# Attention and two expert layers: key tails of two heads in one chunk, sums of values 65 columns a head, and another planned order

## Chip, cores and metric

The kernel runs on one core of a Trainium2 chip. The metric is the device time of one execution in microseconds (us), lower is better. Engines: PE (TensorE matmuls), DVE (VectorE), ACT (ScalarE), POOL (GpSimd), SP (SyncE, which issues most DMAs).

## The reference, cut to what matters

```python
def _attn_ref(q, k, v, omega):          # q, k, v: 4 batches, 8 heads, 576 tokens, 64 wide; omega: 128 x 64
    scale = 1.0 / np.sqrt(np.sqrt(D))
    q_s, k_s = (q * scale, k * scale)
    def phi(x):
        h = np.einsum('bhsd,md->bhsm', x, omega) - np.sum(x * x, axis=-1, keepdims=True) / 2.0
        h = h - np.max(h, axis=-1, keepdims=True)
        return np.exp(h) / np.sqrt(m)
    q_p, k_p = (phi(q_s), phi(k_s))
    kv = np.einsum('bhsm,bhsd->bhmd', k_p, v)
    z = np.sum(k_p, axis=2)
    num = np.einsum('bhsm,bhmd->bhsd', q_p, kv)
    den = np.einsum('bhsm,bhm->bhs', q_p, z)[..., None] + 1e-06
    return num / den
```

Its result, as 2304 rows of 512, goes through two layers of eight experts (512 to 1024, ReLU, back to 512), each row through the expert with the largest gate.

## The kernel before, in words

**Attention** goes by 16 pairs of heads, four to a batch (`class Pair`, L298). A pair's steps are:

- `load_q`, `load_k`, `load_v` (L312 to L340): the inputs, with two heads on the 128 partitions;
- `k_proj` with `features` (L360, L465): keys against omega, 128 tokens at a time, five chunks a head of which the last overlaps the fourth; ten fp32 products with 64 rows each, two heads side by side, into four PSUM banks (tile `ph`); then `nm`, the maximum by DVE, and ten ACT exponentials into `kp`;
- `kv` (L471): for each head five products of `kp` with the values `vt` into `pkv`. A column of ones among the values makes the sum of keys. Three pairs (form R) take 65 columns a head, the others 128;
- `q_split` and `q_proj` (L391, L409): queries against omega. In batches 0 and 1 ("tiled") one load brings both heads and four 64-row fp32 products make both; in batches 2 and 3 each head has a load of its own, is cut into two fp32r parts by a DVE cast and a DVE subtraction, and takes four fp32r products (`pa<-qs`). POOL then makes a maximum over partitions;
- `q_exp`, `q_cut` and `num` (L440, L457, L499): exponentials, and their product with `kv`. Form F keeps fp32 (two matmuls a head, `pa<-qhh,kvr`), form S cuts both sides into fp32r parts (six a head, `qh`, `ql`, `kvh`, `kvl`), form R writes rows instead of columns (`pn`);
- `den_a` to `norm`: division, by way of a small DMA round trip.

An fp32 product shows as two records in the trace, an fp32r product as one.

**Experts.** A `Unit` (L836) is one batch in one layer, with the expert that most of the batch takes. `up` and `down` run 384 fp32r products of 288 columns each (`pm`), eight units in a row: the order is batch 0, batch 1, both in layer 0, then both in layer 1, and the same with batches 2 and 3. Between groups of six such products, at a `slot`, PE takes pieces of attention and of the gates (`gate`, L729: `pg`, `pt`, `pc`, `ptc`). A `Block` gathers 32 rows that need another expert (`pst`, `pxt`, `pu` and others) during the last two units.

**What sets the order.** The program is recorded once, and everything stands in a fixed order on each engine. `Attention.go` (L680) picks the next step by a table of weights (`WEIGHTS`, `RAW_WEIGHTS`, `TWEAKS`, `PACE`), out of those that `Estimate` (L101), a rough clock that runs along, holds to be ready. Where nothing is ready before the first unit, `fill` (L1316) lays down a matmul on zeros (`idle`). From the first unit on, attention and gates share four PSUM banks (`psa`), the units hold the other four (`psm`); ahead of it there are seven. `ORDERS`, `FORMS` and `COPIES` say which unit comes when, which form a pair has, and whether ACT or DVE makes a copy. What is recorded for one engine is worked off strictly in turn.

Of the kernel before, what the change touches and what calls it, by code (L numbers as in the profile page):

```python
# [11 lines left out]
F32 = mybir.dt.float32  # L12
# [13 lines left out]
NCH = 5  # L26
SP = NCH * 128
# [12 lines left out]
MODES = "AAAA"  # L40

TILED = "1100"
# [11 lines left out]
FORMS = "FRRRFFFSSSSSSSSS"  # L54
# [3 lines left out]
WEIGHTS = (-99.0, -99.0, 262.75, -267.46, 198.55, 332.25, -310.29, -471.44, -33.14, 239.82, -489.57, 351.55, -254.05, 173.97)  # L58
RAW_WEIGHTS = (-99.0, -99.0, -374.05, -379.93, 519.94, 42.51, 947.74, -153.49, 153.44, 733.35, -182.45, -952.4, -419.2, -198.78)
# [8 lines left out]
START_PACE = (0.142, 0.015, 7.433)  # L68
START_COPIES = (1, 2, 0, 1, 0, 0, 0)
TWEAKS = {  # L70
    ("den_a", 1): 44.7, ("den_a", 2): 595.6, ("den_a", 3): -18.8, ("den_a", 4): 323.2, ("den_a", 5): 525.4,
    ("den_a", 6): 291.8, ("den_a", 7): -101.8, ("den_a", 8): -71.9, ("den_a", 9): 56.6, ("den_b", 0): 325.6,
    ("den_b", 1): 1.1, ("den_b", 4): 37.9, ("den_b", 5): -9.0, ("den_b", 6): 171.8, ("den_b", 7): 121.2,
    ("den_b", 8): -64.0, ("den_b", 9): -127.0, ("den_c", 0): 75.6, ("den_c", 1): -98.6, ("den_c", 2): 478.0,
    ("den_c", 4): 37.6, ("den_c", 5): -237.6, ("den_c", 6): -550.8, ("den_c", 9): 0.0, ("den_w", 0): 345.4,
    ("den_w", 1): 143.8, ("den_w", 2): 574.5, ("den_w", 3): -16.2, ("den_w", 4): -57.6, ("den_w", 5): -71.8,
    ("den_w", 6): 77.2, ("den_w", 7): 20.5, ("den_w", 8): 24.7, ("den_w", 9): 7.5, ("k_proj", 0): 107.5,
    ("k_proj", 1): -20.1, ("k_proj", 2): 135.6, ("k_proj", 3): -98.0, ("k_proj", 4): -29.4,
    ("k_proj", 5): -51.0, ("k_proj", 6): -49.7, ("k_proj", 8): 473.1, ("k_proj", 9): -623.2, ("kv", 0): -176.7,
    ("kv", 1): -125.4, ("kv", 3): 483.1, ("kv", 4): -62.8, ("kv", 7): -51.7, ("kv", 8): -203.5,  # L80
    ("kv", 9): 650.0, ("norm", 0): 643.8, ("norm", 1): 542.2, ("norm", 2): 77.4, ("norm", 3): -45.2,
    ("norm", 4): -186.2, ("norm", 5): -106.9, ("norm", 6): 227.5, ("norm", 7): 48.0, ("norm", 8): -0.4,
    ("norm", 9): -5.1, ("num", 0): 0.5, ("num", 1): -19.9, ("num", 10): 26.1, ("num", 14): 416.8,
    ("num", 16): 22.8, ("num", 17): 45.6, ("num", 18): 55.1, ("num", 2): -74.7, ("num", 3): 19.4,
    ("num", 4): -844.8, ("num", 6): 170.0, ("num", 7): -558.5, ("q_cut", 1): -198.8, ("q_cut", 11): -85.3,
    ("q_cut", 12): 60.3, ("q_cut", 13): -72.2, ("q_cut", 14): -1186.5, ("q_cut", 16): -207.1,
    ("q_cut", 17): 478.9, ("q_cut", 19): -174.8, ("q_cut", 2): 25.9, ("q_cut", 3): -306.2, ("q_cut", 4): -287.7,
    ("q_cut", 5): -24.0, ("q_cut", 6): -93.1, ("q_cut", 7): -533.3, ("q_cut", 9): -21.1, ("q_exp", 0): -237.5,
    ("q_exp", 1): 916.5, ("q_exp", 10): -245.4, ("q_exp", 11): -365.4, ("q_exp", 13): -179.8,
# [11 lines left out]
class Estimate:  # L101
# [3 lines left out]
    def __init__(self):  # L105
        self.now = dict.fromkeys(("tensor", "vector", "scalar", "gpsimd", "sync", "dma"), 0.7)
        self.written, self.used, self.slots, self.before = {}, {}, {}, {}
        self.sums = set()

        self.window, self.work, self.slow = 0, 0.0, True  # L110

        self.hold = 0.0
# [1377 lines left out]
```

## Time and profile before

| | |
|---|---|
| median of 3 runs | 588.97 us (588.17 to 589.77) |
| profiled execution | 588.86 us, of which the span on the core 587.1 us |
| PE busy | 567.9 us, 97% of the span |
| DVE, ACT, POOL busy | 371.1, 225.3, 68.4 us |
| first expert product | 71.87 us after the start |
| idle matmuls | 54 |

A busy PE is not a PE at its peak: records overlap, so the price of a group is the distance from its start to the next group's start. What stands in brackets in a row of the timeline is idle time of that engine before the row, and what ended it.

### The profile page before, as it was taken

Reading aid. Unit: us, or ns where it says so; the run is one execution under the profiler, and the core shown is the slowest. Engines: PE = TensorE matmul, PEld = TensorE weight load, DVE = VectorE, ACT = ScalarE, POOL = GpSimd, SP = SyncE. Lnnn points to the kernel's source line nnn. Section 1 sums busy time; section 2 is a strip of 40 time slices with the busy share of each in tenths; the row PEclk is TensorE's granted clock in tenths of the full one; section 3 lists DMA queues with packets and bytes.
Section 4 is the critical chain, followed back from the end, with each engine's and each line's share of the span. In section 5 each row is a group of like instructions: output and inputs, shape, how many; then the busy total and the mean of one; then the engine's idle time right before and its main releaser. Section 6 shows DMA issues by size and latency. Waiting matters only on the chain.

```text
span 587.1 us, 11426 instructions
## 1 busy us (share of the span) xinstructions
PE 567.9 (97%) x4519; PEld 540.7 (92%) x4519; DVE 371.1 (63%) x695; ACT 225.3 (38%) x503; POOL 68.4 (12%) x48
## 2 busy tenths in 40 slices
PE   8999989999999999999999999999999999999995
PEld 7887779988999999899999999999999999879995
DVE  4487678887775787487866876764545485313522
ACT  6776645224536224424353344322331232324300
POOL 3670500202001130011201210000000000000000
PEclk9999999989999999999999999999999999999998
DMA  9314376525473263283534634544243238664411
GB/s 315 105 62 129 93 231 194 155 87 171 127 171 123 80 217 89 66 272 130 177 94 124 199 103 114 137 150 136 81 118 133 93 95 250 235 218 154 122 41 45
DMA packets 96955, 82.76 MB, mean 141 GB/s; under 512 B 24576, under 2 KB 78464, under 8 KB 96896
## 3 DMA queue, kind: packets, MB, share of 16 engines
q1 hardware_dynamic: 95776, 81.78, 45.1%
q8 instruction: 37, 0.61, 0.4%
q10 hardware_dynamic: 1120, 0.19, 0.2%
q14 instruction: 22, 0.18, 0.1%
HBM read 66.36 MB, written 15.54 MB: 140 GB/s over the span
## 4 chain that ended last, share of the span: by engine, by line
PE 80%; DVE 8%; DMA 5%; issue 3%; ACT 2%; POOL 0%; SPq 0%; ACTq 0%; DVEq 0%; POOLq 0%
PE pm L208 62%; PE pkv L208 5%; PE ph L208 4%; PE pa L208 4%; DMA wr<-w1a 2%; DVE qhh L208 1%; PE pg L208 1%; DMA wr<-w2a 1%; DVE wl L208 1%; DMA qr<-qT 1%; DVE nm L208 1%; ACT wh L208 1%; PE pby L208 1%; DMA rdd<-dt 1%; ACT kp L208 1%
## 5 line engine op out<-in xcount | busy, mean ns | idle before, releaser
L208 PE MATMUL pm<-xh,wh 128*128 128x288 f32 x512 | 113.4, 303 | 1.6 <-DVE hl L208 1.3
L208 PE MATMUL pm<-hh,wh 128*128 128x288 f32 x512 | 114.2, 302 | 0.6 <-DVE y L208 0.6
L208 PE MATMUL pm<-hh,wl 128*128 128x288 f32 x512 | 111.4, 297 | 0.0
L208 PE MATMUL pm<-hl,wh 128*128 128x288 f32 x512 | 111.3, 297 | 0.0
L208 PE MATMUL pm<-xh,wl 128*128 128x288 f32 x512 | 109.6, 296 | 0.5 <-DVE wl L208 0.5
L208 PE MATMUL pm<-xl,wh 128*128 128x288 f32 x512 | 109.5, 295 | 0.0
L208 POOL PARTITION_ALL_REDUCE qhl<-qhh x32 | 67.2, 2139 | 282.8 <-DVE qhh L208 185.2
L208 ACT CAST wh<-wr 128x1024 fp32r<-128x1024 f32 (+1 forms) x72 | 67.8, 951 | 55.5 <-PE pm L208 40.5
L208 PEld LDWEIGHTS pm<-xh,wh 128*128 128x128 f32 x512 | 82.1, 189 | 5.7 <-DVE hl L208 2.3
L208 PEld LDWEIGHTS pm<-hh,wh 128*128 128x128 f32 x512 | 82.9, 190 | 4.4 <-issue 3.0
L208 DVE TENSOR_TENSOR wl<-wr,wh 128x1024 fp32r<-128x1024 f32 (+1 forms) x72 | 78.5, 1103 | 12.6 <-ACT wh L208 12.2
L208 PEld LDWEIGHTS pm<-hh,wl 128*128 128x128 f32 x512 | 83.3, 190 | 0.0
L208 PEld LDWEIGHTS pm<-hl,wh 128*128 128x128 f32 x512 | 83.2, 190 | 0.0
L208 DVE SCALAR_TENSOR_TENSOR hl<-pm,hh 128x576 fp32r<-128x576 f32 x64 | 48.4, 757 | 54.8 <-ACT hh L208 53.9
L208 PEld LDWEIGHTS pm<-xh,wl 128*128 128x128 f32 x512 | 82.4, 188 | 0.7 <-DVE wl L208 0.7
L208 PEld LDWEIGHTS pm<-xl,wh 128*128 128x128 f32 x512 | 82.3, 188 | 0.0
L208 ACT ACTIVATE hh<-pm 128x576 fp32r<-128x576 f32 x64 | 41.7, 651 | 73.3 <-PE pm L208 73.2
L208 DVE TENSOR_TENSOR y<-pm,cb 128x576 f32<-128x576 f32 (+1 forms) x33 | 24.3, 737 | 58.4 <-PE pm L208 58.3
L208 ACT ACTIVATE kp<-ph,nm 128x128 f32<-128x128 f32 x140 | 38.0, 387 | 21.1 <-DVE nm L208 19.2
L208 ACT ACTIVATE qhh<-qhh 128x576 f32<-128x576 f32 x32 | 22.1, 706 | 58.3 <-DVE qhh L208 56.1
L208 DVE TENSOR_REDUCE nm<-ph 128x3 f32<-128x384 f32 (+1 forms) x64 | 27.2, 484 | 14.2 <-PE ph L208 14.1
L208 PEld LDWEIGHTS pkv<-vt,kp 128*128 128x128 f32 x280 | 32.6, 192 | 1.5 <-ACT ev L208 0.8
(145 smaller groups left out, 580.0 us busy)
## 6 DMA issues: line engine op xcount, KB each, us to landing
wr<-w2a SPq DMA_DIRECT2D x16, 512.0 KB, 4.1
wr<-w2b SPq DMA_DIRECT2D x16, 512.0 KB, 3.9
qr<-qT SPq DMA_DIRECT2D x24, 288.0 KB, 4.3
wr<-w1a SPq DMA_DIRECT2D x12, 512.0 KB, 4.7
wr<-w1b SPq DMA_DIRECT2D x12, 512.0 KB, 3.9
vt<-vp SPq DMA_DIRECT2D x16, 325.0 KB, 4.5
kr<-kT SPq DMA_DIRECT2D x16, 288.0 KB, 4.4
xd<-xraw SPq DMA_DIRECT2D x16, 288.0 KB, 3.5
```

Of the source, the lines that this page charges most:

```text
L208: return f(*args, **kw)
```

## The change

- The last 64 keys of both heads form one chunk: `kT` is laid out with 640 columns, the tail of head 0 on the first 64 partitions and that of head 1 on the others, with zeros elsewhere. `features` makes eight products with 64 rows and one with 128, into three banks; `nm` is made by three reductions, and nine exponentials follow.
- `kv` makes one product of 130 columns for the shared chunk and eight of 65, all into one group of sums; the copies that follow are 130 wide.
- All batches are "tiled": one query load a pair, four 64-row fp32 products, no `q_split`.
- Four pairs (8, 9, 11, 15 of 0 to 15) go from form S to form F.
- `Estimate` follows which PSUM bank will come free next, and prices DMAs and PE's activity otherwise. `go` takes a step only where as many of the shared banks as it needs have a reader recorded: four for `q_proj`, three for `k_proj`, two for `num`, one for `kv`.
- All weights and paces are other numbers; copies go to other engines (`COPIES`). The gates write two exponentials into tiles of their own.

```diff
-NCH = 5
+NCH = 4
+KW = NCH * 128 + 128
-TILED = "1100"
+TILED = "1111"
-FORMS = "FRRRFFFSSSSSSSSS"
+FORMS = "FRRRFFFSFFSFSSSF"
-PACE = (0.097, 0.001, 1.054, 1.126, 886.024, 3.696, 0.265, 0.264, 1.069, 256.941, 0)
-COPIES = (1, 1, 2, 1, 0, 0, 2)
+PACE = (0.168, 0.007, 0.458, 0.787, 1760.614, 1.248, 1.538, 0.278, 0.307, 366.477, 149.2)
+COPIES = (1, 0, 0, 1, 0, 0, 0)
-START_COPIES = (1, 2, 0, 1, 0, 0, 0)
+START_COPIES = (0, 0, 0, 2, 0, 1, 2)
...
+    def spare(self, pool, tag):
+        ring = id(pool), tag
+        return pool.bufs - sum(n not in self.seen or self.seen[n][1] for n in self.slots.get(ring, ()))
...
         def features(self, x, out):
-            parts = [(cs, self.heads(len(cs) * NF)) for cs in ((0, 1, 2), (3, 4))]
+            parts = [(ps, slice(NCH * j, NCH * j + NCH)) for j, ps in enumerate(self.heads(NCH * NF))]
+            for c in range(NCH):
+                for j, (ps, _) in enumerate(parts):
+                    r = slice(64 * j, 64 * j + 64)
+                    nc.tensor.matmul(
+                        ps[:, c * NF : (c + 1) * NF], x[r, c * 128 : c * 128 + 128], om[r, :], start=True, stop=True
+                    )
+            ps = pl.psa.tile([128, 512], F32, tag="pa", name="ph")[:, :NF]
+            nc.tensor.matmul(ps, x[:, NCH * 128 : KW], om, start=True, stop=True)
...
         def kv(self):
+            pkv = pl.psa.tile([128, 512], F32, tag="pa", name="pkv")[:, :VW]
+            nc.tensor.matmul(pkv, self.kp[:, 2 * NCH], self.vt[:, NCH], start=True, stop=False)
             for j in range(2):
+                w = slice((HD + 1) * j, (HD + 1) * (j + 1))
                 for c in range(NCH):
                     nc.tensor.matmul(
-                        o, self.kp[:, c, j * NF : (j + 1) * NF], self.vt[:, c, v], start=c == 0, stop=c == NCH - 1
+                        pkv[:, w], self.kp[:, NCH * j + c], self.vt[:, c, w], start=False, stop=j == 1 and c == NCH - 1
                     )
...
+        def banks(self, kind, p):
+            if kind == "q_proj":
+                return 4 if p.tiled else 2
+            return {"k_proj": 3, "num": 2, "kv": 1, "norm": 2 * p.raw}.get(kind, 0)
...
                 if any(now[e] > now["tensor"] + limit for e in engines):
                     continue
+                if est.spare(pl.psa, "pa") < self.banks(kind, self.pairs[k]):
+                    continue
```

**Where the order moves.** On PE among the expert products, where a query head of batch 2 or 3 is projected, the list of before reads:

```order
L208 MATMUL pm<-hh,wl 128x288 x2
L208 MATMUL pa<-qs,omsth 128x288
L208 MATMUL pa<-qs,omstl 128x288
L208 MATMUL pa<-qs,omsth 128x288
L208 MATMUL pa<-qs,omstl 128x288
L208 MATMUL pm<-hh,wh 128x288 x2
```

and a pair of these batches in the list of after, right behind a `num` in form S (the last two rows of which stand first):

```order
L237 MATMUL pa<-qh,kvl 128x288
L237 MATMUL pa<-ql,kvh 128x288
L237 MATMUL ph<-qr,om 128x288 x4
L237 MATMUL pm<-hh,wh 128x288 x2
L237 MATMUL pm<-hl,wh 128x288 x2
```

Sixteen short groups on two banks each, two a pair, have become eight groups of four fp32 products on four banks, one a pair. All of them stand among the expert products, before and after.

On PE behind the gate's transposes `pt` of batch 1, `k_proj` follows at once in both. Before:

```order
L208 MATMUL pt<-ident,lg 72x128 x2
L208 MATMUL ph<-om,kr 128x128 x10
L208 MATMUL pm<-hh,wh 128x288 x2
L208 MATMUL pm<-hl,wh 128x288 x2
L208 MATMUL pm<-hh,wl 128x288 x2
```

and after:

```order
L237 MATMUL pt<-ident,lg 72x128 x2
L237 MATMUL ph<-om,kr 128x128 x9
L237 MATMUL pm<-hh,wh 128x288 x2
L237 MATMUL pm<-hl,wh 128x288 x2
L237 MATMUL pm<-hh,wl 128x288 x2
```

The place is the same; with the bank of `pt` the step holds four banks where it held five.

On PE between the first gate's products `pg` and the first expert product, before (17 matmuls on zeros follow, and then `pm`):

```order
L208 MATMUL pkv<-vt,kp 128x128 x10
L208 MATMUL pg<-xraw,wg_93 32x144 x16
L208 MATMUL ph<-om,kr 128x128 x10
L208 MATMUL pt<-ident,lg 72x128 x2
L208 MATMUL pa<-qhh,kvr 128x288 x4
L208 MATMUL pc<-g,ones 128x64
L208 MATMUL ph<-qr,om 128x288 x4
L208 MATMUL pkv<-vt,kp 128x128 x10
```

and after, from `pc` on:

```order
L237 MATMUL pc<-g,ones 128x64
L237 MATMUL ph<-qr,om 128x288 x4
L237 MATMUL pkv<-vt,kp 128x130
L237 MATMUL pkv<-vt,kp 128x65 x8
L237 MATMUL ph<-om,kr 128x128 x9
L237 LDWEIGHTS zeros
L237 MATMUL idle<-zeros 128x256
L237 LDWEIGHTS zeros
L237 MATMUL idle<-zeros 128x256
L237 MATMUL pm<-xh,wh 128x288 x2
```

A ninth `k_proj` has moved ahead of the first unit, `pg` has moved ahead of the seventh `kv`, and of the 17 matmuls on zeros two are left.

On ACT ahead of the first weight casts of the first unit (`wh<-wr`), after:

```order
L237 ACTIVATE ge<-g 72x64
L237 ACTIVATE te<-gt 72x8
L237 CAST kvh<-pkv 128x130
L237 ACTIVATE kp<-ph,nm 128x128 x9
L237 CAST wh<-wr 128x512 x2
L237 CAST wh<-wr 128x1024
```

and before:

```order
L208 ACTIVATE g<-g 72x64
L208 ACTIVATE gt<-gt 72x8
L208 CAST kvh<-pkv 128x256
L208 DMA dt<-xraw 16x1x36
L208 DMA dt<-ev 16x1x36
L208 CAST wh<-wr 128x512 x2
```

The nine exponentials of that ninth `k_proj` now stand ahead of the first cast.

## Rows read from the trace of the kernel before

**Rows 1.** The page: busy time, share of the span and instructions of each engine.
```profile
PE 567.9 (97%) x4519; PEld 540.7 (92%) x4519; DVE 371.1 (63%) x695; ACT 225.3 (38%) x503; POOL 68.4 (12%) x48
```
**Rows 2.** The page: the chain that ended last, by engine.
```profile
PE 80%; DVE 8%; DMA 5%; issue 3%; ACT 2%; POOL 0%; SPq 0%; ACTq 0%; DVEq 0%; POOLq 0%
```
**Rows 3.** Stretches before and from the first expert product: length, then busy time by engine.
```profile
0.00:71.87 71.87, 68.21 (x574) 56.66 (x574) 45.72 (x104) 49.79 (x156) 33.73 (x32) 1.00 0.42 137
71.87:588.00 516.13, 499.64 (x3946) 484.03 (x3946) 325.34 (x592) 175.55 (x348) 34.70 (x17) 0.99 0.46 141
```
**Rows 4.** PE's timeline in the first stretch: start, length, group, records.
```profile
31.19 1.24 PE L208 MATMUL ph<-qr,om 64*128 64x288 f32 x8
32.37 2.45 PE L208 MATMUL pkv<-vt,kp 128*128 128x65 f32 x20
34.74 1.39 PE L208 MATMUL ph<-om,kr 64*128 64x128 f32 x20
...
41.73 2.45 PE L208 MATMUL pkv<-vt,kp 128*128 128x128 f32 x20
...
53.76 1.24 PE L208 MATMUL pa<-qhh,kvr 128*128 128x288 f32 x4
54.83 0.80 PE L208 MATMUL pf<-ident,xt 128*128 128x128 f32 x5
```
**Rows 5.** PE's timeline among the expert products.
```profile
108.17 0.30 PE L208 MATMUL pa<-qs,omsth 128*128 128x288 f32 x1
...
108.70 0.43 PE L208 MATMUL pm<-hh,wh 128*128 128x288 f32 x2
...
182.19 0.29 PE L208 MATMUL pa<-qh,kvh 128*128 128x288 f32 x1
...
182.99 0.42 PE L208 MATMUL pm<-hh,wh 128*128 128x288 f32 x2
...
183.87 1.39 PE L208 MATMUL ph<-om,kr 64*128 64x128 f32 x20
185.18 0.40 PE L208 MATMUL pm<-hh,wh 128*128 128x288 f32 x1
```
**Rows 6.** PE's timeline: the three long waits inside a `k_proj`.
```profile
125.60 0.71 PE L208 MATMUL ph<-om,kr 64*128 64x128 f32 x6 [1.34 <-ACT kp L208]
...
143.75 0.71 PE L208 MATMUL ph<-om,kr 64*128 64x128 f32 x6 [1.09 <-ACT kp L208]
...
236.19 0.71 PE L208 MATMUL ph<-om,kr 64*128 64x128 f32 x6 [1.35 <-ACT kp L208]
```
**Rows 7.** A stretch behind the first of them; the number 0.54 is the granted clock.
```profile
126.00:129.70 3.70, 3.70 (x19) 3.58 (x17) 3.42 (x8) 1.61 (x7) 0.00 (x0) 0.54 0.11 17
```
**Rows 8.** PE's timeline in that stretch.
```profile
126.24 0.84 PE L208 MATMUL pm<-hh,wh 128*128 128x288 f32 x2
...
129.56 0.57 PE L208 MATMUL pm<-hh,wh 128*128 128x288 f32 x2
```
**Rows 9.** Timeline of DVE and PE where the `Block` begins.
```profile
495.79 0.81 DVE L208 SCALAR_TENSOR_TENSOR sel<-pos,state,sel 128x576 f32<-128x576 f32 x1
...
496.70 0.61 PE L208 MATMUL pst<-ident,sel 128*96 128x128 f32 x4 [1.24 <-issue]
```
**Rows 10.** PE's timeline from the first gate to the first expert product.
```profile
59.92 1.19 PE L208 MATMUL pg<-xraw,wg 128*32 128x144 f32 x32
...
65.49 0.36 PE L208 MATMUL pc<-g,ones 72*128 72x64 f32 x2
...
69.72 2.02 PE L208 MATMUL idle<-zeros 128*128 128x256 bf16 x17
...
71.87 0.54 PE L208 MATMUL pm<-xh,wh 128*128 128x288 f32 x2
```
**Rows 11.** ACT's timeline there.
```profile
63.20 2.68 ACT L208 ACTIVATE kp<-ph,nm 128x128 f32<-128x128 f32 x10
...
71.20 1.26 ACT L208 CAST wh<-wr 128x512 fp32r<-128x512 f32 x2 [0.90 <-DMA wr<-w1a]
```

More of the change, by code (lines that the diff above doesn't have):

```diff
@@ L122, in tile @@
         if len(names) >= bufs:
-            self.before[t.tensor.name] = names[-bufs]
+            old = names[0]
+            if self.banks.get(ring):
+                read = [n for n in names if n in self.seen and not self.seen[n][1]]
+                old = min(read, key=lambda n: self.seen[n][0], default=old)
+            names.remove(old)
+            self.before[t.tensor.name] = old
         names.append(t.tensor.name)
+    def spare(self, pool, tag):
+        ring = id(pool), tag
+        return pool.bufs - sum(n not in self.seen or self.seen[n][1] for n in self.slots.get(ring, ()))
     def clock(self, begin):
@@ L141, in run @@
         if op == "dma_start":
-            self.now[engine] = begin + (0.45 if out.shape[0] % 128 == 0 or out.shape[0] < 64 else 0.65)
-            end = self.now["dma"] = max(begin + 1.1, self.now["dma"]) + math.prod(out.shape) * 4 / 330e3
+            self.now[engine] = begin + (0.42 if out.shape[0] % 128 == 0 else 0.55)
+            row = out.shape[-1] * 4
+            cost = math.prod(out.shape[:-1]) / 16e3 * (2 + row / 25 if row >= 512 else 40 if row > 256 else 10)
+            if len(out.shape) > 2 and row >= 512 or out.shape[0] == 64:
+                cost *= 1.5
+            end = self.now["dma"] = max(begin + 1.1, self.now["dma"]) + max(0.17, cost)
             end += 1.0
@@ L156, in run @@
             rows = 64 if ins[-1].shape[0] == 64 else 32 if out.shape[0] == 32 else 128
-            if rows != self.rows:
+            turn = rows != self.rows
+            if turn:
                 begin += 0.1
@@ L160, in run @@
                 self.rows = rows
-            cost *= self.clock(begin)
-            self.work += cost
+            busy = cost
+            if op != "transpose" and ins[-1].dtype == F32:
+                busy = 4 * n / 2400 * cost / (2 * max(2 * n / 2400 + 0.002, 0.111) + (0.107 if turn else 0))
+            clock = self.clock(begin)
+            cost *= clock
+            self.work += busy * clock
             end = self.now[engine] = begin + cost
@@ L179, in run @@
                 tail = 0.083
-                if self.hold - 1.2 < begin < self.hold and not psum:
-                    begin = self.hold
+                for h in self.holds:
+                    if h < begin < h + 1.2 and not psum:
+                        begin = h + 1.2
             else:
@@ L488, in kv @@
[L488 to L497 removed]
+            kvh = pl.ap.tile([128, VW], F32 if self.whole else F32R, tag="kvh", name="kvh")
@@ L499, in num @@
+            nc.scalar.copy(out=kvh, in_=pkv)
+            self.kvs = (kvh,)
+            if not self.whole:
+                kvl = pl.ap.tile([128, VW], F32R, tag="kvl", name="kvl")
+                nc.vector.tensor_tensor(out=kvl, in0=pkv, in1=kvh.bitcast(F32), op=ALU.subtract)
+                self.kvs = kvh, kvl
         def num(self, j):
@@ L688, in go @@
                 engines = engines.split()
-                if kind == "norm" and self.pairs[k].raw or kind == "q_exp" and self.pairs[k].flip:
+                if kind == "norm" and self.pairs[k].raw:
                     engines = ["tensor", *engines]
```

197 lines of the change are left out of this document (82 added, 115 removed).

## The prediction

> **What bounds the kernel now.** I read the page first: PE is busy 97% of the span and no other engine above 63% [rows 1], and the chain of work that ended last lies on PE for 80% [rows 2]. Busy records overlap, so I then took the timeline, where a group's price is the distance to the next start. Six fp32r products of 288 columns, the shape of the expert products, take 0.80 us (182.19 to 182.99) [rows 5], 0.133 each, and from 71.87 us on PE is busy 499.6 of the span's remaining 515 us [rows 3]. There the time is a sum of PE's groups plus the few stalls in the timeline. The first 71.87 us are different: PE has 68.2 us of records there [rows 3], but a part of them are matmuls on zeros, and the end of the stretch is set by the chain gate, choice of the expert, weight load, cast [rows 10, 11]. So I price the change as (a) PE's groups, (b) stalls that go or come, (c) the first stretch.
>
> **(a) The groups on PE.**
> *Sums of values.* Each of 16 pairs has nine products in place of ten, and 65 columns in place of 128 in 13 of them. A group of twenty records with 65 columns takes 32.37 to 34.74, 2.37 us, and its length, 2.45, is the very length of a group with 128 columns [rows 4]. So fewer columns give nothing, and one product of two records gives 2.37/10 = 0.24; as the hand-over to the next group stays, I take 0.225. For 16 pairs 3.6 us, half of it in the first stretch: -1.8 among the expert products.
> The Trainium skill (TensorE: Matmul & The Clock Gate, Back-to-back issue gap) has the spacing of isolated matmuls follow their columns, and so would make the narrow products nearly half as dear; the same page (LDWEIGHTS) has the weight load go by the stationary columns, which are 128 in both. The rows go with the second.
> *Keys.* Before: ten products with 64 rows, two side by side, so five steps. After: four steps of that kind and one product on all 128 rows, five steps again; the turn from 64 to 128 rows, which came at the group's end, now comes inside it. I take 0. The bounds are -0.3 and +0.2 a pair: one step of the twenty records' 1.31 us [rows 5] is 1.31/5 = 0.26, and an extra turn cannot be dearer than such a step.
> *Queries of batches 2 and 3.* Two groups of 0.53 us (108.17 to 108.70) [rows 5], together 1.06, become one of 1.18 (31.19 to 32.37) [rows 4]. That row contains the turn out of the 64-row form; the turn into it hides in the group ahead. Bounds +0.12 and +0.33 a pair; I take +0.25, nearer the upper, since here 128-row products stand on both sides. Eight pairs: +2.0.
> *Four pairs from form S to F.* A head costs 0.80 in form S (182.19 to 182.99) [rows 5] and 1.07 in form F (53.76 to 54.83) [rows 4]. Four pairs with two heads: 8 x 0.27 = +2.1.
> So among the expert products PE's groups come out at -1.8 + 2.0 + 2.1 = +2.3 us, not below zero. What these edits save lies on DVE (16 query casts with 16 subtractions, eight `ql`) and in eight query loads; with 325 and 176 us busy in 516 [rows 3], DVE and ACT hide that, and it counts only where a wait names them. The 11% larger key loads run far ahead; cover gone, they cost what the first cast's wait for a weight load costs, 0.90 [rows 11].
>
> **(b) Stalls.**
> *Waits inside `k_proj`.* Three of eight such groups among the expert products stop after 14 of 20 records, until ACT has read exponentials out of a bank: 1.34, 1.09, 1.35 us [rows 6]. They want four banks of four, at places where `pt`, `ptc` or `pkv` still holds one. After, the step wants three, and `go` counts the banks whose reader is recorded: in the same place behind `pt`, three and one make four. I take all 3.8 us as gone.
> *Granted clock.* Behind the first of them the clock fell to 0.54 of full in the mean of 3.7 us [rows 7], that is to 1.2 GHz in most of it. Twelve expert products, with the small `pc` among them, took from 126.24 to 129.56, 3.32 us [rows 8], where 12 x 0.133 = 1.6 was due, and a little for `pc`. PE had been idle 1.34 us, with the 64-row group around it. I take this as gone too: -1.6.
> *Start of the Block.* The first `pst` waits 1.24 us for `sel` on DVE [rows 9]. DVE's list is the same there, but PE's has 180 expert products between the last `ptc` and `pst` where it had 162: 18 x 0.133 = 2.4 us later, more than the wait. -1.2.
> *New waits.* The tiled query group wants all four shared banks, right behind a `num` in three places, and its four copies out now all go to ACT. Bounds: 0, and a wait as long as `k_proj`'s in each of eight, 8 x 1.3 = 10. The copies start while the group still runs, and expert products, which use other banks, mostly follow; so nearer the lower: 0.2 each, +1.6. The waits of the first unit and other small ones I leave as they are.
>
> **(c) The first stretch.** By the lists, ahead of the first expert product stand one more `k_proj` (+1.3), eight shorter `kv` (-1.8) and 43 matmuls on zeros in place of 54 (seventeen take 2.02 [rows 10], so eleven 1.3: -1.2). PE alone would be done 1.7 us earlier. The gate's `pg` has one `kv` less ahead of it, so it can come 2.4 + 6 x 0.225 = 3.7 us earlier than 59.92, if ACT and DVE keep up; some of that is given back, as one more `kv` and `k_proj` stand between `pg` and `pt`. Against it: nine exponentials of the added `k_proj` stand ahead of the first weight cast on ACT, and ten take 2.68 us [rows 11]. Before, PE had 6.4 us from `pc` to the first expert product [rows 10]; after, `q_proj`, `kv` and `k_proj` take 1.2 + 2.1 + 1.3 = 4.6 of it, and then reductions on DVE, nine exponentials (2.4) and half of the casts (0.6) follow, while PE has two matmuls on zeros: about 8 us. So PE stands some 3 us there. Bounds for the first expert product: 68.2 and 74. I take 71.0: -0.9. The `k_proj` made early is no longer due later: -1.5 (1.31 and a turn).
>
> **Sum.** +2.3 - 3.8 - 1.6 - 1.2 + 1.6 - 0.9 - 1.5 = -5.1 us. Against the profiled execution, 588.86 (1.8 more than its span), this is 583.8; the median of the runs is 0.1 higher, so I say **583.9**.
>
> **Rivals.**
> *Slower: query groups wait for ACT.* If each of the eight tiled groups, with four banks to empty by one engine, waits behind a weight cast or other work as `k_proj` did, 1.3 us each, that is 10 in place of 1.6, and one fall of the clock adds 1.6: 593.9. It ends above the old time once a group loses more than 0.85 us. For it: the waits of [rows 6] had this cause, on ACT, with fewer banks wanted. Against: `go` now asks for four banks whose readers are recorded, and ACT has 340 of 516 us free [rows 3].
> *The bank waits stay.* A recorded reader need not have run: where ACT is behind, three banks wait as four did. Then 3.8 + 1.6 come back: 589.3.
> *A late first unit.* The standstill ahead of the first expert product lasts 2 us longer and the clock falls behind it for 1.6: 587.5. For it: the exponentials ahead of the cast.
> *An early one.* The gate's 3.7 us come through: 580.7.
> *Narrow products stream cheaper.* If a record's 0.118 us followed its columns, 65 in place of 128 would save 0.058 on 13 x 16 records, 12 us: 571.8. By the Trainium skill's gap rule, named above, it would come out so; the equal rows of 65 and 128 columns speak against it.
>
> **How the numbers follow.** Forecast 0.60, slower queries 0.10, bank waits stay 0.10, late first unit 0.10, early first unit 0.07, narrow products 0.03. A measurement can tell about 0.3%, 1.8 us: 587.2 to 590.7 is no change. Faster: nearly all of the forecast, the early unit, the narrow products and half of the late unit, 0.74; slower: the first rival and a little of the second, 0.11; the rest, 0.15, the same. The range takes in the forecast, the late unit, the remaining bank waits and most of the early unit: 580 to 589.3.
>
> **What would show it.** Right: `k_proj` groups without idle time inside; no fall of the clock behind 100 us; no wait of `pst`; first expert product near 71; query groups near 1.2 to 1.4 us; a 65-column group of 18 records near 2.1. Wrong: idle time on PE that names ACT's copies of queries (`qhh`); a first expert product behind 73; 65-column records closer than 0.1 us.

## The result, and the profile after

The changed kernel takes **582.44 us** (median of four runs, 580.46 to 583.69) beside 588.57 us for the kernel before: a ratio of **0.9891, with an interval of 0.9862 to 0.9920**, some 6.4 us less. The forecast was 583.9. The profiled execution took 582.52 us, its span is 580.7 us. Some executions of one and the same kernel take 1.5% or more longer than its quickest one, and the medians and ratios in this document leave them out. The time came out close to the forecast; two of the steps to it did not, and that they cancelled is luck.

The page of the kernel after: busy time by engine, and the chain that ended last, by engine. They answer [rows 1] and [rows 2].

```profile
PE 563.9 (97%) x4428; PEld 531.2 (91%) x4428; DVE 326.7 (56%) x625; ACT 225.6 (39%) x489; POOL 66.1 (11%) x48
...
PE 88%; DVE 6%; ACT 2%; DMA 2%; issue 1%; ACTq 0%; SPq 0%; DVEq 0%
```

PE is busy 97% again, now 4.0 us less, and the chain lies on it for 88% instead of 80%. DVE lost 44 us of work and ACT stayed the same; neither is busy for more than 56% of the span.

The stretches ahead of and from the first expert product on, as in [rows 3] (length, then busy time of PE, PE's weight loads, DVE, ACT and POOL, granted clock, DMA share, GB/s):

```profile
0.00:74.88 74.88, 67.13 (x548) 54.58 (x548) 50.33 (x127) 43.42 (x133) 32.88 (x32) 1.00 0.49 166
74.88:580.70 505.82, 496.73 (x3880) 476.66 (x3880) 276.38 (x499) 182.21 (x357) 33.19 (x16) 1.00 0.45 135
```

The first stretch got **3.0 us longer** (71.87 to 74.88), where the prediction had it 0.9 shorter. The rest, from the first expert product to the end of the span, fell from 515.2 to 505.8 us, **9.4 less**, where the prediction's terms gave 4.2 less.

PE's timeline where the first stretch ends (start, length, engine, line, operation, tiles, shapes, records, idle time ahead and who ended it), to be read beside [rows 10]:

```profile
65.59 0.44 PE L237 MATMUL pc<-g,ones 72*128 72x64 f32 x2 [0.49 <-DVE g L237]
...
67.12 2.22 PE L237 MATMUL pkv<-vt,kp 128*128 128x130 f32 x18
69.28 1.58 PE L237 MATMUL ph<-om,kr 64*128 64x128 f32 x18
70.69 0.38 PE L237 MATMUL idle<-zeros 128*128 128x256 bf16 x2
74.88 0.85 PE L237 MATMUL pm<-xh,wh 128*128 128x288 f32 x2 [3.81 <-ACT wh L237]
...
76.49 0.32 PE L237 MATMUL ptc<-ident,g 72*64 72x72 f32 x1
...
78.32 0.42 PE L237 MATMUL pm<-xl,wh 128*128 128x288 f32 x2
```

and ACT's there, beside [rows 11]:

```profile
71.90 2.43 ACT L237 ACTIVATE kp<-ph,nm 128x128 f32<-128x128 f32 x9 [1.02 <-DVE nm L237]
74.16 2.14 ACT L237 CAST wh<-wr 128x512 fp32r<-128x512 f32 x3
```

PE runs out of work at 70.9 and stands 3.81 us. On ACT the nine exponentials of the ninth `k_proj` come first, then the two casts of the first expert's weights. Behind that wait the granted clock is at half, 1.2 GHz, as the window shows (0.50 is the granted clock):

```profile
74.50:77.90 3.40, 3.02 (x12) 2.95 (x13) 2.83 (x5) 2.01 (x4) 0.00 (x0) 0.50 0.50 179
```

From 74.88 to 78.32 us there are fourteen expert products and `ptc`, 3.44 us, where 14 x 0.133 and 0.1 would be 1.96: the slow clock cost 1.5 us.

Among the expert products, the place behind `pt` where [rows 6] had the first of the long waits, a query group, the first `pst`, and the two largest waits that are left:

```profile
134.33 0.41 PE L237 MATMUL pt<-ident,lg 128*72 128x128 f32 x2 [0.47 <-ACT lg L237]
134.67 1.58 PE L237 MATMUL ph<-om,kr 64*128 64x128 f32 x18
136.01 0.51 PE L237 MATMUL pm<-hh,wh 128*128 128x288 f32 x2
```

```profile
203.76 1.24 PE L237 MATMUL ph<-qr,om 64*128 64x288 f32 x8
204.94 0.53 PE L237 MATMUL pm<-hh,wh 128*128 128x288 f32 x2
```

```profile
492.80 0.60 PE L237 MATMUL pst<-ident,sel 128*96 128x128 f32 x4
```

```profile
236.51 0.23 PE L237 MATMUL ptc<-ident,g 72*64 72x72 f32 x1 [0.90 <-DVE g L237]
```

```profile
342.22 0.25 PE L237 MATMUL ptc<-ident,g 72*64 72x72 f32 x1 [0.91 <-DVE g L237]
```

The `k_proj` behind `pt` runs through (134.67 to 136.01, 1.34 us), and so do the other six, each of which stands behind expert products and not behind `pt`, `ptc` or `pkv`. `pst` no longer waits. What is new are two transposes of the gate, `ptc`, that wait 0.90 and 0.91 us for DVE.

**How a wait is priced here.** The idle time in brackets is shorter than what a wait costs, since it starts only at the modelled end of the record ahead. I take the distance from the start of that record's group to the next start, less the usual distance. The kernel before, PE's timeline in its three stalled `k_proj` groups ([rows 6] has the second half of each, [rows 8] the product behind the first):

```profile
123.10 1.16 PE L208 MATMUL ph<-om,kr 64*128 64x128 f32 x14
```

```profile
141.19 1.48 PE L208 MATMUL ph<-om,kr 64*128 64x128 f32 x14
...
144.39 0.53 PE L208 MATMUL pm<-hh,wh 128*128 128x288 f32 x2
```

```profile
233.69 1.16 PE L208 MATMUL ph<-om,kr 64*128 64x128 f32 x14
...
236.83 0.53 PE L208 MATMUL pm<-xh,wh 128*128 128x288 f32 x2
```

123.10 to 126.24, 141.19 to 144.39 and 233.69 to 236.83 are 3.14, 3.20 and 3.14 us, where an undisturbed group took 1.31 [rows 5]. The three waits cost 5.5 us, not the 3.8 in the brackets. In the same way `pst` cost 1.4 (bracket 1.24).

The kernel before also waited four times in its first unit, which the prediction left as it was:

```profile
73.17 0.53 PE L208 MATMUL pm<-xh,wl 128*128 128x288 f32 x2 [0.50 <-DVE wl L208]
...
76.69 0.75 PE L208 MATMUL pa<-qhh,kvr 128*128 128x288 f32 x2 [0.62 <-ACT xraw L208]
...
81.80 0.43 PE L208 MATMUL pm<-xh,wl 128*128 128x288 f32 x2
83.53 0.53 PE L208 MATMUL pm<-xh,wh 128*128 128x288 f32 x2 [1.30 <-DVE hl L208]
```

and a fourth, of 0.51, at 100.36. By distances they are 3.6 us: the third, for one, takes 1.73 from 81.80 to 83.53 where 0.27 is usual, 1.46; the others come to 0.66, 0.85 and 0.66. After, none of the four is there: no bracket stands on PE between 74.88 and 134.33 us.

From the first expert product on, in us:

| step | forecast | measured |
|---|---|---|
| three waits inside `k_proj` | -3.8 | -5.5 |
| slow clock behind the first of them | -1.6 | -1.6 |
| slow clock behind the first unit's wait | 0 | +1.5 |
| `pst` | -1.2 | -1.4 |
| four waits in the first unit | 0 | -3.6 |
| waits that came (`ptc` 1.05 and 1.07, `pt` 0.63) less two small ones that went (1.3) | +1.6 | +1.45 |
| one `k_proj` made earlier | -1.5 | -1.5 |
| sums of values | -1.8 | -1.8 |
| queries | +2.0 | +2.4 |
| four pairs in form F | +2.1 | +1.4 |
| sum | -4.2 | -8.65 |

The stretch itself gives -9.4 (-8.9 with the repeated run below, 506.3 us); 0.7 us of it is in no row of this table. The last four rows before the sum are group prices: the time from the last expert product ahead of a group to the second one behind it, less 3 x 0.133, which takes in the turns at both ends.

### The profile page after: what moved, and what is told of

The parts are those of the page before. It is cut to its first block, busy times and chain, and to the rows that moved or that the text cites. A ratio compares the mean times of both kernels' runs of the same rounds, so it can differ in the third digit from the quotient of the medians.

```text
span 580.7 us, 11112 instructions
## 1 busy us (share of the span) xinstructions
PE 563.9 (97%) x4428; PEld 531.2 (91%) x4428; DVE 326.7 (56%) x625; ACT 225.6 (39%) x489; POOL 66.1 (11%) x48
## 4 chain that ended last, share of the span: by engine, by line
PE 88%; DVE 6%; ACT 2%; DMA 2%; issue 1%; ACTq 0%; SPq 0%; DVEq 0%
PE pm L237 66%; PE ph L237 6%; PE pkv L237 5%; PE pa L237 4%; PE pg L237 1%; PE pn L237 1%; ACT kp L237 1%; PE pby L237 1%; DVE hl L237 1%; DMA om<-omst 1%; DVE nm L237 1%; DMA rb<-rdd 1%; DMA dt<-ev 1%; DVE y L237 0%; DVE qhh L237 0%
## 5 line engine op out<-in xcount | busy, mean ns | idle before, releaser
L237 POOL PARTITION_ALL_REDUCE qhl<-qhh x32 | 64.9, 2066 | 212.2 <-ACT qhh L237 117.0
L237 PEld LDWEIGHTS pkv<-vt,kp 128*128 128x128 f32 x288 | 34.0, 194 | 2.2 <-issue 0.9
L237 PE MATMUL pkv<-vt,kp 128*128 128x65 f32 (+1 forms) x288 | 34.9, 276 | 0.0
L237 DVE TENSOR_REDUCE nm<-ph 128x4 f32<-128x512 f32 (+1 forms) x48 | 23.8, 551 | 18.8 <-PE ph L237 18.8
```

Of the source, the lines that this page charges most:

```text
L237: return f(*args, **kw)
```

## The experiments

Ratios are to the kernel before, run beside it on the same chip. One run of a kernel can differ from the next by 2 us and more, in the start of the first stretch above all (see the last section), so times are medians and single waits are read from rows.

### The changed kernel once more

> The changed kernel once more, unaltered, beside the two that follow. By its first runs: 582.4, ratio 0.989; a ratio outside 0.986 to 0.992 would say that figures of different days can't be set side by side.

582.35 us, ratio 0.9878 (0.9841 to 0.9915). The figure holds, and kernels that were measured at other times can be set beside it.

### Do three banks remove the waits in `k_proj`?

The theory is that a group of three banks finds room where one of four had to wait. The rival: the order moved, and any order of this length might have had room. So the order is kept and the fourth bank is given back, in all sixteen groups, and then only in the seven among the expert products. Each such group also has one more maximum on DVE.

```diff
+            fourth = pl.psa.pool.tile([128, 512], F32, tag="pa", name="ph")[:, :NF]
...
+                    real = fourth if j == 1 and c == NCH - 1 else o
...
+                for lo, hi, src in ((0, 3, ps[:, : 3 * NF]), (3, 4, fourth)) if n == 1 else ((0, m, ps),):
```

> The changed kernel with its order of instructions kept, in which each k_proj group holds four banks instead of three: the fourth chunk of the second head goes to a bank of its own, and its maximum is taken by a VectorE instruction of its own (one more a group, some 0.2 to 0.4 us there). Theory: that a k_proj group found a bank still held is what cost the kernel before 1.34, 1.09 and 1.35 us inside three groups, and the changed kernel is free of it because it needs one bank less than there are; with four, waits inside groups come back where the logits, a kv group or a query group held one shortly before: at one to four places among the expert products, 1 to 2 us each, so 584 to 588. Rival: the waits went because the order moved, and the changed kernel's order has room for a fourth bank: no wait inside a k_proj group, 582 to 583.

588.4 us, ratio 0.9990 (0.9966 to 1.0014): 6 us above the changed kernel. The one profile of this kernel, of an execution of 597.5 us, has a single wait inside a `k_proj`, behind `pt`:

```profile
149.45 0.80 PE L237 MATMUL ph<-om,kr 128*128 128x128 f32 x2 [1.95 <-ACT kp L413]
```

None of the nine groups of the first stretch waits in it. The second variant leaves those nine alone.

> The changed kernel with its order kept, in which only the seven k_proj groups that stand among the expert products hold a fourth bank (the last chunk of the second head in a bank and a maximum of its own); the nine ahead of them are as in the changed kernel. It sizes what the fourth bank costs among the expert products alone. Theory: one group finds a bank held, the one behind the logits' transposition (134.67 us of the changed kernel, no wait in it), and waits 1.3 to 2 us inside it; if the granted clock falls behind that wait another 1 to 1.5 us are lost: 584 to 586.5, ratio 0.992 to 0.996. Rival: the loss of the first variant lay in the groups ahead of the expert products, and this one is at 582.4 to 583.5.

584.8 us, ratio 0.9930 (0.9902 to 0.9957), 2.4 us above the changed kernel. PE's timeline behind `pt`:

```profile
135.09 1.16 PE L399 MATMUL ph<-om,kr 64*128 64x128 f32 x16
138.20 0.49 PE L237 MATMUL ph<-om,kr 128*128 128x128 f32 x2 [1.95 <-ACT kp L415]
138.45 0.51 PE L237 MATMUL pm<-hh,wh 128*128 128x288 f32 x2
```

The group that took 1.34 us takes 3.36 (135.09 to 138.45); it stops ahead of its ninth product until ACT has read the exponentials out of a bank, which is what [rows 6] showed at the very same place. It is the only `k_proj` with a wait in it. The theory's mechanism is shown at this one place, and its price, 2.0 us, is nearly the whole difference of the medians. The granted clock did not fall this time (1.00 from 138.2 to 142 us). The rival holds for the rest: with four banks the other six groups still run through, so two of the three waits of the kernel before, 3.7 of the 5.5 us, went with the order. Before, one stood right behind `ptc` (at 233.69) and one behind `ptc` and `pkv` (at 141.19); in the changed order no `k_proj` stands behind these. The other 3.6 us of the first variant are not shown to come from the banks; where they come from stays open.

One clause of the prediction falls here without a run: that `go` now asks for banks whose readers are recorded. With these two lines taken out, the lists of all five engines are row for row the same. In this plan they refuse nothing; what removed the waits is, behind `pt`, the third bank in place of the fourth, and elsewhere the order.

### What sets the late start?

**The nine exponentials, by holding the group back.** 

```diff
             if kind == "k_proj":
+                if k == 8 and pl.psi is not None:
+                    return None
```

> The changed kernel in which the k_proj group that stands last ahead of the first expert product (its eighteen products at 69.28 us, its nine exponentials on ScalarE from 71.90 to 74.33 us, ahead of the cast of the first expert's weights at 74.16) is held back until the first expert product has begun; the planner then fills TensorE's wait with idle products. Theory: those nine exponentials set the end of the 3.81 us wait; without them the cast ends by 71.5 and the first expert product is issued at 71.0 to 71.9, as in the kernel before, and of the 3 us won there part is given back, because the waits for the first experts' weights that the kernel before had from 73 to 101 us (2.9 us in four gaps) return: total 580.9 to 583.5. Rival A: no payback, total 579 to 579.5. Rival B: the first expert's weights, not ScalarE, arrive late: the first expert product stays at 74.5 or later.

```profile
70.29 0.53 PE L237 MATMUL pm<-xh,wh 128*128 128x288 f32 x2 [0.78 <-ACT wh L237]
...
72.93 0.53 PE L237 MATMUL pm<-xh,wl 128*128 128x288 f32 x2 [1.84 <-DVE wl L237]
```

The first expert product comes at 70.29, so without the nine exponentials the start is early, and rival B falls. But the total is 588.3 us, ratio 0.9986 (0.9967 to 1.0005), 6 us above the changed kernel: 1.84 us come back at once as a wait for `wl` on DVE, and the planner's order moved further on, with new waits of 1.75 us (148.03, for a weight cast) and 1.24 us (159.24). With so much moved, the run says what set the start and not what an early start is worth.

**The same exponentials, by ACT's order alone.** In this kernel the maxima and exponentials of that group (`tail`) are issued later. It leaves PE's order as it is and puts the two casts ahead of the nine exponentials on ACT, and on DVE the two `wl` ahead of the three maxima.

```diff
+                late = pl.psi is not None and att.n["k_proj"] == 9
...
+                held.append(tail)
...
             lead(n)
             if n == 0:
+                for t in held:
+                    t()
```

> The changed kernel with one exchange on ScalarE and VectorE: the two casts of the first expert's weights (and VectorE's two subtractions behind them) stand ahead of the nine exponentials (and the three maxima) of the last k_proj group before the first expert product, instead of behind them. TensorE's order is the same. Theory: the nine exponentials, 2.43 us, and the 1.02 us that ScalarE waited for their maxima set the late start; the first expert product is issued 2.3 to 3.3 us sooner in its stretch, TensorE stands 1 to 2 us instead of 3.81, and of that gain at most half is given back to late weights: total 579.5 to 581.5. Rival A: the later weights set the pace of the first expert whatever the start, as in the kernel before: 582 to 583. Rival B: the wait is for the first expert's transfer: the first product stays where it was.

586.5 us, ratio 0.9952 (0.9934 to 0.9970), 4.1 us **above** the changed kernel. All three expectations are wrong. The kernel built on it, with 12 matmuls on zeros ahead of the first expert product and two gate transposes made later, shows why:

> The exchange of the casts with the exponentials as above, 12 idle products (1.3 us) on TensorE ahead of the first expert product so that it doesn't stand before them, and two transpositions of the gate (at 236.51 and 342.22 us of the changed kernel, which wait 0.90 and 0.91 us for VectorE) put one group of three expert products later; no other engine's order moves. Theory: 1.8 us from the two transpositions, 1 to 3 us from the start, a clock that does not fall: 577 to 579.5. Rival: VectorE's late row moves on to who reads the transposition, and the start is paid back: 581 to 582.4.

584.3 us, ratio 0.9932 (0.9910 to 0.9954); 577 to 579.5 was expected. PE and ACT there:

```profile
76.73 0.85 PE L237 MATMUL pm<-xh,wh 128*128 128x288 f32 x2 [6.08 <-ACT kp L423]
```

```profile
70.70 0.62 ACT L237 CAST wh<-wr 128x512 fp32r<-128x512 f32 x1 [0.59 <-DMA wr<-w1a]
74.23 2.44 ACT L423 ACTIVATE kp<-ph,nm 128x128 f32<-128x128 f32 x9 [2.92 <-DVE nm L419]
```

Both casts are done at 71.3, and PE still stands 6.08 us, until the last exponential ends at 76.7: the row names `kp`, not `wh`. My theory that the casts' place on ACT alone set the start fell. The first expert product writes to banks 0 and 1 in the recorded program and that last `k_proj` to 2, 3 and 4, so it isn't that bank either. What is left is the place where the first stretch's banks are closed (seven, and one for the matmuls on zeros) and the same eight opened anew for the units: a bank opened there waits for the last reader of all that were closed. (Of the two transposes that this kernel was to move, I had moved one that did not wait in place of the one at 342.22; at 236.51 no wait is left in the row, at the other 0.91 stayed.)

**The closed banks.** So the next kernel closes them ahead of the last `k_proj` group and lets that group take new ones (`held` has the whole group here, with its maxima and exponentials):

```diff
             if n == 0:
+                for _ in range(16):
+                    nc.tensor.engine.matmul(idle, zeros[:, 0:128], zeros, start=True, stop=True)
                 pl.psi = None
                 psums.close()
                 pl.psm = pool(ctx, "psm", 2, space=PSUM)
                 pl.psa = pool(ctx, "psa", 4, space=PSUM)
+                for t in held:
+                    t()
```

> The changed kernel, in which the seven banks of the first stretch are closed and the six of the expert stretch opened ahead of the last k_proj group instead of behind it; that group takes its banks from the new ones. So the first expert product does not wait for that group's exponentials, on ScalarE the two casts of the first weights stand ahead of them, and 16 idle products (1.8 us) stand ahead of the group, since it now has to wait for the readers of the closed banks. Orders are otherwise the same. Theory (the first expert product waits for the last reader of any bank that was closed, and the casts stood behind the same exponentials): the k_proj group starts at about 71.2 us, the first expert product is issued 1.5 to 2.5 us sooner than in the changed kernel, the clock does not fall: total 578.5 to 580.5. Rival (what is won at the start is given back to late weights): 582 to 583.

```profile
69.25 1.58 PE L409 MATMUL ph<-om,kr 64*128 64x128 f32 x18
70.58 0.51 PE L237 MATMUL pm<-xh,wh 128*128 128x288 f32 x2
...
72.60 0.53 PE L237 MATMUL pm<-xh,wl 128*128 128x288 f32 x2 [1.25 <-DVE wl L237]
```

The first expert product is issued at 70.58, 3.3 us ahead of the first of those exponentials on ACT (73.84): it no longer waits for them, so in this order the closed banks are shown to be the cause. In the changed kernel both causes hold: the exponentials end at 74.33, and the first cast behind them just ahead of 74.88. Beside the changed kernel's repeated run (72.89, and the same pace at the start) it comes 2.3 us sooner, and the granted clock does not fall (1.00 from 70 to 78 us). Against this, 1.25 us go into a wait for `wl`, on DVE, and 0.35 into one at 83.48; from the first expert product to the end it takes 507.2 us beside 506.3. The profiled spans are 577.8 and 579.2 us; the medians 581.85 and 582.35, ratio 0.9862 (0.9825 to 0.9899). The total forecast, 578.5 to 580.5, was missed, and no gain in the total is shown beyond the spread of the runs. An earlier start is worth at most a part of what it gains.

**Paying a late start back.** In the kernel before, 28 matmuls on zeros, 3.1 us, ahead of the first expert product:

```diff
             lead(n)
             if n == 0:
+                for _ in range(28):
+                    nc.tensor.engine.matmul(idle, zeros[:, 0:128], zeros, start=True, stop=True)
```

> The kernel before with 28 more idle products, some 3.1 us, in TensorE's program right ahead of the first expert product; nothing else is moved. It gives the kernel before the late start that the changed kernel has (74.88 instead of 71.87 us) without the changed kernel's other parts. Theory: from 73 to 101 us the kernel before waits 2.9 us in four gaps for weights and transfers that are late; with a start 3 us later those gaps go, and the late start pays itself back: 588.6 to 589.3, ratio 1.000 to 1.001. Rival: those gaps depend on something else than the start, and the 3 us are added: 591.5 to 592, ratio 1.005.

588.95 us, ratio 0.9999 (0.9984 to 1.0014): 3.1 us more on PE cost between -0.9 and +0.8. The theory's number holds, its account of the place does not: in the profiled run the first expert product comes at 74.12, and the waits of 73.17 and 76.69 are gone, but the one of 83.53 stays, the one of 100.36 is longer (1.09), and one of 0.81 is new at 97.99.

```profile
84.47 0.53 PE L208 MATMUL pm<-xh,wh 128*128 128x288 f32 x2 [1.30 <-DVE hl L208]
```

That run was the slowest of the twelve (592.19) and won nothing back: from the first expert product to the end it takes 516.3 us, the kernel before 515.2. Where the others won the time back stays open.

### What does the slow clock behind the wait cost?

```diff
             if n == 0:
+                for _ in range(34):
+                    nc.tensor.engine.matmul(idle, zeros[:, 0:128], zeros, start=True, stop=True)
```

> The changed kernel with 34 more idle bf16 products (operands of zeros, 0.11 us each in a row at 2.4 GHz, some 3.6 us) in TensorE's program right ahead of the first expert product; every other instruction stays where it was. In the changed kernel TensorE stands 3.81 us there, and its granted clock is 0.5 from 74.5 to 77.9 us, with the first expert products 0.24 us apart instead of 0.13. Theory: the idle products end about when the wait for ScalarE's cast ends (74.88 us), the clock does not fall, the products from 74.9 to 77.9 run at 0.13 us each, and the run ends 1.2 to 1.6 us sooner: about 581.0, ratio to the kernel before 0.987. Rival: the fall of the clock is paid back, since the expert products then catch up with their weights' transfers or with ScalarE: 582.4, no difference.

```profile
75.38 0.52 PE L237 MATMUL pm<-xh,wh 128*128 128x288 f32 x2
```

```profile
75.30:78.70 3.40, 3.32 (x23) 3.13 (x24) 2.97 (x5) 1.71 (x4) 0.00 (x0) 1.00 0.61 217
```

580.38 us, ratio 0.9854 (0.9829 to 0.9879), 2.0 us below the changed kernel. The granted clock stays at 1.00 where it was 0.50. From the first expert product to `pt` the profiled execution takes 58.3 us (75.38 to 133.66) where the changed kernel took 59.5 (74.88 to 134.33), 1.2 less, and to the end 504.8 where it took 505.8: the theory's lower end, and it isn't paid back within that run. In the totals the runs of the two kernels overlap (579.6 to 582.9 and 580.5 to 583.7), so they alone don't exclude the rival's zero. PE had no work for those 3.8 us with or without the zeros; what the zeros buy is the clock behind them.

### Do 65 columns cost as much as 128?

```diff
-                        pkv[:, w], self.kp[:, NCH * j + c], self.vt[:, c, w], start=False, stop=j == 1 and c == NCH - 1
+                        o, self.kp[:, NCH * j + c], self.vt[:, c, 2 * j : 2 * j + 128], start=j == 0 and c == 0, stop=False
```

> The changed kernel with its order of instructions kept, in which the eight products of each kv group that are 65 columns wide are 128 columns wide (the columns beyond the head's 65 are left unread), and the shared chunk's product, 130 columns in two parts of 65, comes last of the nine instead of first. Theory: a 4-byte product with its own stationary data takes 0.112 us in a row whether it is 65 or 128 columns wide (0.112 a record in the group of eight at 59.82 of the changed kernel, 0.111 a record in the groups of ten of 128 columns before), so the time stays at 582.4, within 1. Rival, by the rule of the Trainium skill (TensorEngine page, on back-to-back gaps by free size) that a narrower product is issued sooner: some 57 groups of eight products, each product longer by up to the 63 columns at 4 passes, 0.026 to 0.105 us, make 12 to 48 us, so 594 or more.

```profile
57.07 2.28 PE L237 MATMUL pkv<-vt,kp 128*128 128x128 f32 x18
59.28 1.58 PE L237 MATMUL ph<-om,kr 64*128 64x128 f32 x18
```

581.49 us, ratio 0.9875 (0.9850 to 0.9901). Eighteen records take 2.21 us to the next start with 128 columns, and 2.16 with 65 (67.12 to 69.28 in the changed kernel). Between these widths a group's time goes by the count of its products and not by their columns. The rival's sum was wrong: there are 16 such groups and not 57, so its 0.026 to 0.105 us a product make 3.4 to 13.4 us for 128 products, and 585.8 or more. The four runs lie between 581.4 and 583.3, so it is out all the same. It went by the gap rule of the Trainium skill (TensorE: Matmul & The Clock Gate, Back-to-back issue gap), by which a narrower product is issued sooner; this trace does not agree.

### `pst` alone

```diff
+            for _ in range(3):
+                yield ()
```

> The kernel before with one edit of the change alone: the first transposition of the selection is put three groups of expert products later. Theory: its wait of 1.24 us at 496.70 us goes, nothing else moves by more than one group, and the run ends 1.2 to 1.4 us sooner, 587.2 to 587.4, ratio 0.9977. Rival: what follows the selection was late anyway, and the wait comes back further on: within 0.3 us of before.

```profile
496.48 0.60 PE L208 MATMUL pst<-ident,sel 128*96 128x128 f32 x4
```

The wait is gone and does not come back there: 586.71 us, ratio 0.9956 (0.9936 to 0.9975), 2.7 us less. That is more than the 1.4 us that the wait cost; the interval's end, 1.5, just misses it. In this run the waits of 76.69 and 100.36 were absent too, though nothing in the edit touches them, and a `ptc` waited 0.70 instead. I count the 1.4 as shown and the rest as open.

### A version that beats both

The kernel with the closed banks, and the two `ptc` that wait, each made at the generator's next step:

```diff
-        nc.tensor.transpose(ptc, g[:, 5].rearrange("p c e -> p (c e)"), ident[:TW, :TW])
+        put_off = (l, b) in ((1, 1), (0, 3)) and not again
...
         yield [ptc]
+        if put_off:
+            nc.tensor.engine.transpose(ptc, gt_, one)
         nc.scalar.copy(out=ct, in_=ptc)
```

> The kernel with the banks closed ahead of the last k_proj group, and the two transpositions of the gate that wait 0.90 and 0.91 us for VectorE (at 236.51 and 342.22 us of the changed kernel) six expert products, 0.8 us, later on TensorE; no other engine's order moves. Theory: 0.8 us less at each, 1.6 us less than without them: 577 to 579. Rival: the reader of the transposed rows is late instead: no difference to the kernel without them.

579.1 us, ratio **0.9827** (0.9778 to 0.9875), the lowest median here, some 10 us below the kernel before. The profiled span is 576.3 us beside 577.8 without the two moved transposes: 1.5 less, as forecast, and the reader of the transposed rows is not late. Moving a product that waits 0.9 us by six expert products of 0.8 us is enough.

## Why the prediction was right, and where it was not

**Right in part, and too small.** All three waits inside `k_proj` went. Behind `pt` it is because the group takes three banks: with a fourth, in two kernels, a wait of 1.95 us stands there again. The other two, 3.7 us by distances, don't come back with four banks; they went with the order, which the prediction did not say. The term was mis-sized: 3.8 us were read from the brackets, where the distances of [rows 5, 6] would have given 5.5. The `pst` term is right (1.2 forecast, 1.4 by distances).

**Right in kind and size.** Sums of values: 2.16 us a group, a step of 0.21 to 0.24, no gain from fewer columns; "near 2.1" was forecast. Keys: a group of nine products takes 1.34 and, with the turn, the same 1.51 as one of ten. Queries: a group takes 1.18 to the next start (203.76 to 204.94), as [rows 4] said; with the products around it 1.37, so +0.30 a pair where +0.25 was taken, within the bounds. Form F is cheaper than forecast: two heads in a row take 1.73 us (138.96 to 140.69), 0.97 a head with the products around them, so +0.17 where +0.27 was taken. The row in [rows 4] had a group alone in the first stretch, with the turn into another kind of product behind it.

**Wrong: the first stretch.** The prediction saw that the nine exponentials would stand ahead of the casts and that PE would stand "some 3 us"; it stood 3.81. But 71.0 for the first expert product meant `pc` at 63.0 and 8 us behind it. `pc` came at 65.59 (63.58 in the repeat, whose start ran quicker), since little of the 3.7 us that the gate's products were to come forward arrived there: `pg` came 2.4 us sooner (57.54), but `pt`, with one more `kv` and `k_proj` ahead of it, 0.9 later (63.31). And 9.3 us lay behind it (65.59 to 74.88): `q_proj`, `kv` and `k_proj` took 5.1 (4.6 taken), and from the end of PE's work to the first expert product it was 4.2 (3.4 taken). I also gave half a cause: not ACT's order alone, but also the banks closed at that point, which wait for the same exponentials. In the repeat the first expert product comes 1.0 us later than before and not 3.0, so 2.0 of the 3.0 are the spread of the start.

**Wrong: the clock.** The fall behind the `k_proj` wait is gone, as forecast, but one came behind the first unit's wait, 1.5 us, as the rival "late first unit" had it. PE stood 0.8 us longer than forecast where that rival had 2; its fall of the clock came true, and its time, 587.5, did not.

**Missed: the first unit's waits.** "The waits of the first unit I leave as they are": they cost 3.6 us, and all four went, which pays for the delay. What the late start has to do with it is shown in part only. The waits of 73.17 and 76.69, 1.5 us, go where the start alone is late, and an early start brings a wait for `wl` back (1.84 and 1.25 us); but the one of 76.69 and the one of 100.36 were also absent in a run of the kernel before with only `pst` moved, whose first expert product came at 71.45. The product that waited at 100.36 was of the old query groups and is gone. The largest, 1.46 us at 83.53, stays where the start alone is late, and is absent in the kernel with the closed banks, which starts at 70.58: it went with the order on ACT. Before, `hh`, which `hl` needs, stood behind an exponential that waits for DVE; after, it stands first and waits for PE's products alone:

```profile
81.46 0.69 ACT L208 ACTIVATE qhh<-qhh 128x576 f32<-128x576 f32 x1 [1.64 <-DVE qhh L208]
82.05 0.63 ACT L208 ACTIVATE hh<-pm 128x576 fp32r<-128x576 f32 x1
```

```profile
79.84 0.65 ACT L237 ACTIVATE hh<-pm 128x576 fp32r<-128x576 f32 x1 [2.73 <-PE pm L237]
```

The term should not have been put at nothing: a new start and a new order on ACT cannot leave these waits unchanged.

**Wrong: where the new waits are.** 1.6 us were put on the query groups; none of the eight waits. The 2.75 us that came are at `ptc` and `pt`. The rival of 593.9 had its cause in those query groups and is out. The narrow products (571.8) are out by rows and by a run. The rival of an early first unit should have read 581.1 and not 580.7, since 0.9 of its 3.7 us were in the forecast already.

So -5.1 came out as -6.4 with errors of +3.9 in the first stretch and -5.2 behind it. The mechanisms priced in (a) and most of those in (b) held; that the total came so close is luck.

## What to carry to other kernels

Price a wait by the distance between starts, not by the idle time shown, and count what a group holds (here banks) at the place where it stands: one bank less was worth 2 us at a single place, and nothing at the six others. A later start of a stretch can change the waits behind it, so price the start and those waits as one term, and ask of each wait which row it hangs on: the largest of four here hung on ACT's order and not on the start. Where an engine must stand for some us, look at its clock behind the wait; and where buffers are closed and opened anew, look for what is still being read: the first product here waited 6.08 us for the reader of a bank that it did not write to.

## What was not expected of the hardware

The start of the first stretch differs from run to run of one order. PE's first query group took 2.29 us in the changed kernel and the group at 14.84 us took 1.24; in its repeat the group at 7.16 already ran at the quick pace for part of it:

```profile
7.10 2.29 PE L237 MATMUL ph<-qr,om 64*128 64x288 f32 x8
...
14.84 1.24 PE L237 MATMUL ph<-qr,om 64*128 64x288 f32 x8
```

```profile
7.16 1.64 PE L237 MATMUL ph<-qr,om 64*128 64x288 f32 x8
```

```profile
72.89 0.85 PE L237 MATMUL pm<-xh,wh 128*128 128x288 f32 x2 [3.81 <-ACT wh L237]
```

With that the first expert product moved from 74.88 to 72.89 us, and the spans are 580.7 and 579.2.

Some small rows on DVE take four to seven times as long while POOL's all-reduce runs. In the kernel with the banks closed early, POOL is in it from 68.08 to 72.0 us, and there:

```profile
69.23 0.83 DVE L237 TENSOR_SCALAR gt<-gt 72x8 f32<-72x8 f32 x1
70.10 1.09 DVE L237 SCALAR_TENSOR_TENSOR gt<-te,gt 72x8 f32<-72x8 f32 x1
71.12 0.21 DVE L237 TENSOR_TENSOR g<-g,prim 72x64 f32<-72x64 f32 x1
```

0.83 and 1.09 us, where the same two rows took 0.17 and 0.16 us at 342 us in a kernel in which POOL was idle there; the next row, still within POOL's, is as short as ever, 0.21. The two rows stand ahead of `wl` on DVE in that kernel, for which PE waits 1.25 us, and in the changed kernel a row of 0.88 us (235.49, POOL is in an all-reduce from 235.15) stands ahead of the `ptc` at 236.51. That POOL is the cause is read from the coincidence alone.
